# Gated attention and MLP decode: the last product in four column groups of one result row each, copied into one row of 512

## Chip, cores and metric

The kernel runs on 1 core of a Trainium2 chip. The metric is the device time of one execution in microseconds (us); before the change it is 189.38 us (median of 3 runs).

## What is computed

One token of width 512 goes through two branches, which a gate mixes. Branch a is attention with 32 heads of width 128 over a cache of 4096 positions; branch b is an MLP of 1376 units with a squared ReLU. All tensors are bfloat16.

```python
g = sigmoid((x * gate_w).sum(-1, keepdims=True))
q = (x @ wq).reshape(1, 1, 32, 128).transpose(0, 2, 1, 3)
p = softmax(einsum("bhqd,bhkd->bhqk", q, k_cache) * 128 ** -0.5)
o = einsum("bhqk,bhkd->bhqd", p, v_cache)
a = o.transpose(0, 2, 1, 3).reshape(1, 1, 4096) @ wo        # wo: 4096 x 512
r = maximum(x @ w1 + b1, 0)
b = (r * r) @ w2 + b2
out = g * a + (1 - g) * b                                   # 512 numbers
```

## The kernel before

The instructions of each engine are written out by hand, one block for each (SP, GpSimd, ScalarE, TensorE, VectorE), and semaphores order them. The heads are treated in eight groups of four (`NQ = 8`); a group's keys or values are one load of 4 MB, 128 partitions with 32 KB each. SP issues all large loads (wq, w1, w2, the keys and values, and last wo) in one order, each as soon as its buffer is free.

For a group, TensorE transposes a part of the keys (L427), ScalarE copies them, and TensorE forms scores (L441); GpSimd (L313) and VectorE (L680, L689, L695) form the other scores by products and sums. Then come the maximum, the exponentials (L358), the product with the values (L470) and a step that sorts the heads' results out (`extract`, L479). The MLP is computed in the first group's turn.

The steps that matter here are at the ends of the blocks.

- wo lies in SBUF as 128 partitions of 32 rows (`wo_sb[:, t, :]`, t = 0 to 31, 512 columns each). SP loads it in `NW` = 4 pieces, with the bounds `TS`: rows 0-19, 20-27, 28-30 and 31, each with a semaphore of its own (L293).
- `regroup` (L541) and a VectorE copy (L744) bring the attention result, times the gate, into columns: column t of `o2` belongs to row t of wo. `o2` is the middle of three columns per t in `o2p`; the outer two are zeros.
- `accs` are the accumulators of the output, in one PSUM bank (`pX`): two tiles of 2 partitions x 128 columns, at partitions 32 and 0. Column block j of the output (j = 0 to 3) belongs to tile j % 2, and there to partition j // 2. A matmul with a slice of two columns, one of them zero (`o2p[:, t, 1 - j // 2:3 - j // 2]`), adds to one of the two partitions and zero to the other. The bias (L520), the MLP's result (`mlp_cols`, L535) and the rows of wo are added there; for the first two the slice comes from `pick2`, three columns with the middle one set.
- `attn_rows` takes the rows of wo: rows 0 to `WW` - 1 = 15 as one matmul of 512 columns each (L551) into row 0, 32, 64 or 96 of the bank `pO`, and rows 16 to 31 as four matmuls of 128 columns (L557) into `accs`. VectorE copies `pO` to `pvf` (L746), and `wide_rows` (L566) adds its four rows into `accs`, ahead of row 20.
- `busy` (L573) issues matmuls whose results are not used; there are several in the last 17 us, one of them ahead of `wide_rows`.
- After the last matmul VectorE copies tile 0 (L748) and ScalarE tile 1 (L385), each 2 x 128, into `ob`, two partitions of 256, and SP stores these as two rows of 512 bytes (L296).

Of the kernel before, what the change touches and what calls it, by code (L numbers as in the profile page):

```python
# [5 lines left out]
def bass_gated_mix__gqa_block_cached__dense_activation_squared_relu__decode_kernel(  # L6
# [14 lines left out]
    fp32 = mybir.dt.float32  # L21
    i32 = mybir.dt.int32
    bf16 = mybir.dt.bfloat16
    ALU = mybir.AluOpType
    ACT = mybir.ActivationFunctionType
    AX = mybir.AxisListType

    NH = 32
# [39 lines left out]

    TS = [0, 20, 28, 31, 32]
    NW = len(TS) - 1  # L70
    WW = 16


    k_p = A_k_cache.rearrange("a h (q b) d -> (a h q) (b d)", b=NB)
# [2 lines left out]
    wo_v = A_wo.rearrange("(p t) n -> p (t n)", t=32)  # L77
    w1_v = B_w1.rearrange("(p t) n -> p (t n)", t=4)
    w2_v = B_w2[0:F0, :].rearrange("(p g) n -> p (g n)", g=FG)
    out_v = out[0, 0, :].rearrange("(j p) -> j p", p=256)  # L80
    w2_x = B_w2[F1:F, :].rearrange("(q t) n -> q (t n)", t=TX)

    ctx = ExitStack()
    with ctx:
        def sb(name, shape, dt):
            return ctx.enter_context(nc.sbuf_tensor(name, shape, dt))
# [4 lines left out]
        def sem(name):  # L91
            return ctx.enter_context(nc.semaphore(name))
# [8 lines left out]
        wo_sb = WO.rearrange("p (t n) -> p t n", t=32)  # L101
        kT = sb("kT", [128, NR, TC * 128], bf16)
# [9 lines left out]
        grow = sb("grow", [1, DM], bf16)  # L112
        b1r = sb("b1r", [1, F], bf16)

        ob = kT[:, 1, 0:256]
        xcol = sb("xcol", [128, 4], bf16)
        sel = sb("sel", [NH, 4, 128], bf16)
        oT = sb("oT", [NH, 128], bf16)
        o2p = sb("o2p", [128, NH, 3], bf16)
        o2 = o2p[:, :, 1]  # L120
        ident = sb("ident", [128, 128], bf16)
        identf = sb("identf", [128, 128], fp32)
        pick = sb("pick", [128, 4, 60], fp32)
        pvf = sb("pvf", [112, 512], fp32)
# [20 lines left out]
        b2r = Kt[0:1, 2, 14 * 1024:14 * 1024 + DM]  # L145
        b2g = Kt[0:1, 2, 15 * 1024:16 * 1024].bitcast(fp32)

        pick2 = sb("pick2", [112, 3], fp32)

        TT = pb("T", [128, NT * 512], fp32)  # L150
        T = [TT[:, i * 512:(i + 1) * 512] for i in range(NT)]
# [2 lines left out]
        pO = pb("pO", [128, 512], fp32)  # L154
        pM = pb("pM", [128, 512], fp32)
        pX = pb("pX", [128, 512], fp32)
# [5 lines left out]
        SL = pS[0:NH, 0:256].bitcast(bf16)  # L162
        H = pX[:, 160:160 + FN + TX]

        accs = [pX[32:34, 0:128], pX[0:2, 0:128]]
        O = pX[0:NH, 288:416]

        QT = pX[:, :].bitcast(bf16).rearrange("p (j d) -> p j d", d=128)
# [66 lines left out]
        s_wm = sem("s_wm")  # L235
        s_hw = sem("s_hw")
        s_mc = sem("s_mc")
        s_wc = sem("s_wc")
        s_ww = sem("s_ww")
        s_hv = sem("s_hv")  # L240
        s_hs = sem("s_hs")
        s_acc = sem("s_acc")
        s_fin = sem("s_fin")
        s_out = sem("s_out")
# [8 lines left out]
        @on(nc.sync)  # L253
        def _(eng):
            def load_k(i):
                if i >= NK:
                    eng.wait_ge(s_t, CB[i - NK + 1])
                    eng.wait_ge(s_mu, XP * (i - NK + 1))
                    eng.wait_ge(s_pm, GP * (i - NK + 1))  # L259
                if i == 2:  # L260
                    eng.wait_ge(s_ml, 1)
                eng.dma_start(Kt[:, i % NK, :], k_p[i * 128:(i + 1) * 128, :]).then_inc(s_k[i % NK], 16)

            def load_v(i):
                if i == 1:
                    eng.wait_ge(s_qr, NQ)
                    eng.wait_ge(s_h, 2)
                if i < NQ - 2:
                    if i >= NV:
                        eng.wait_ge(s_pv, i - NV + 1)  # L270
                    eng.dma_start(VT(i), v_p[i * 128:(i + 1) * 128, :]).then_inc(s_v[i % NV], 16)
                    return
                eng.wait_ge(s_t, CB[i])
                eng.wait_ge(s_mu, XP * i)
                eng.wait_ge(s_pm, GP * i)
                eng.dma_start(VT(i), v_p[i * 128:(i + 1) * 128, :]).then_inc(s_vl[i - (NQ - 2)], 16)  # L276

            load_k(0)
            eng.dma_start(w1_sb, w1_v).then_inc(s_w1, 16)
            eng.dma_start(w2a, w2_v).then_inc(s_w2, 16)  # L280
            for r in range(4):
                eng.dma_start(WX[r:QX:4, :], w2_x[r:QX:4, :]).then_inc(s_w2, 16)
            load_k(1)
            load_v(0)
            load_k(2)
            for i in range(NQ):
                if i >= 1:
                    load_v(i)
                if i + LAG < NQ:
                    load_k(i + LAG)  # L290
            eng.wait_ge(s_pv, NQ - 3)
            for c in range(NW):
                eng.dma_start(WO[:, TS[c] * DM:TS[c + 1] * DM], wo_v[:, TS[c] * DM:TS[c + 1] * DM])\  # L293
                   .then_inc(s_wo[c], 16)
            eng.wait_ge(s_fin, 2)
            eng.dma_start(out_v, ob[32:34, :]).then_inc(s_out, 16)  # L296
            eng.wait_ge(s_out, 16)

        @on(nc.gpsimd)
# [19 lines left out]
        def _(eng):  # L319
# [62 lines left out]
                    neg_max(i - 1)  # L382
                    exps(i - 1)
            eng.wait_ge(s_acc, 1)
            eng.activation(ob[32:34, 128:256], accs[1], ACT.Copy).then_inc(s_fin, 1)  # L385

        @on(nc.tensor)
        def _(eng):
            eng.wait_ge(s_id, 2)
            for c in range(4):  # L390
                mm = eng.transpose(SL[:, c * 128:c * 128 + 128], ident[:, c:128:4], ident[:, :])
            mm.then_inc(s_sl, 1)
            eng.wait_ge(s_x, 32)
            for t in range(4):
                mm = eng.matmul(XC[:, t:t + 1], xrow[:, t:DM:4], ident[0:1, 0:1], start=True, stop=True)
# [12 lines left out]
            for j in range(NQ):  # L408
                if j >= NT:
                    wait_q(eng, j - NT)  # L410
                for t in range(4):
                    mm = eng.matmul(T[j % NT][:, :], xb[:, t, :], wq_sb[:, t, j * 512:(j + 1) * 512],  # L412
                                    start=(t == 0), stop=(t == 3))
# [99 lines left out]
            def mlp_out():  # L513
                eng.wait_ge(s_w2, 16 * 5)
                eng.wait_ge(s_hs, 1)

                eng.wait_ge(s_wm, 3)
                eng.wait_ge(s_g, 4)
                for j in range(4):
                    eng.matmul(accs[j % 2], pick2[0:1, 1 - j // 2:3 - j // 2], b2g[:, j * 128:j * 128 + 128],  # L520
                               start=(j < 2), stop=False, skip_group_check=True)
                for n in range(FN + TX):
                    if n < FG:
                        rhs = w2a[0:height(n), n * DM:(n + 1) * DM]
                    else:
                        rhs = WX[:, (n - FN) * DM:(n - FN + 1) * DM]
                    r = 32 * (n % 4)
                    mm = eng.matmul(pO[r:r + 1, :], hs[0:height(n), n:n + 1], rhs, start=(n < 4),
                                    stop=(n >= FN + TX - 4))
                mm.then_inc(s_ml, 1)  # L530

            def mlp_cols():
                eng.wait_ge(s_mc, 1)
                for j in range(4):
                    eng.matmul(accs[j % 2], pick2[:, 1 - j // 2:3 - j // 2], pvf[0:112, j * 128:j * 128 + 128],  # L535
                               start=False, stop=False, skip_group_check=True)

            def regroup():
# [7 lines left out]
            def attn_rows(c):  # L546
                eng.wait_ge(s_wo[c], 16)
                for t in range(TS[c], TS[c + 1]):
                    r = 32 * (t % 4)
                    if t < WW:  # L550
                        mm = eng.matmul(pO[r:r + 1, :], o2[:, t:t + 1], wo_sb[:, t, :], start=(t < 4),  # L551
                                        stop=(t >= WW - 4), skip_group_check=True)
                        if t == WW - 1:
                            mm.then_inc(s_ww, 1)
                        continue
                    for j in range(4):
                        mm = eng.matmul(accs[j % 2], o2p[:, t, 1 - j // 2:3 - j // 2],  # L557
                                        wo_sb[:, t, j * 128:(j + 1) * 128], start=False,
                                        stop=(t == 31), skip_group_check=True)
                if c == NW - 1:  # L560
                    mm.then_inc(s_acc, 1)

            def wide_rows():
                eng.wait_ge(s_wc, 1)
                for j in range(4):
                    eng.matmul(accs[j % 2], pick2[:, 1 - j // 2:3 - j // 2], pvf[:, j * 128:(j + 1) * 128],  # L566
                               start=False, stop=False, skip_group_check=True)

            def busy(n):
                for u in range(n):
                    eng.matmul(T[0][:, :], ident[:, :], kT[:, 0, 0:512], start=True, stop=True,  # L573
                               skip_group_check=True)
# [39 lines left out]
            regroup()  # L614
            busy(2)
            for c in range(NW):
                if c == 1:
                    busy(1)
                    wide_rows()
                attn_rows(c)  # L620

        @on(nc.vector)
        def _(eng):
# [9 lines left out]
                              identf[:, :].rearrange("p (c r) -> p c r", c=4)[:, :, 0:16]  # L633
                              .rearrange("p c (b h) -> p b h c", b=4), AX.X, ALU.add).then_inc(s_ho, 1)
            eng.memset(E[:, :, :, :], 0.0).then_inc(s_ho, 1)
            eng.memset(pick2[:, :], 0.0).then_inc(s_wm, 1)
            eng.memset(o2p[:, :, :], 0.0).then_inc(s_wm, 1)
            eng.wait_ge(s_ho, 7)
            eng.wait_ge(s_wm, 2)
            eng.tensor_copy(pick2[:, 1:2], pick[0:112, 0, 28:29]).then_inc(s_wm, 1)  # L640
            eng.wait_ge(s_sl, 1)
            eng.tensor_copy(sel[:, :, :], SL.rearrange("h (c m) -> h c m", c=4)).then_inc(s_ho, 1)
            eng.wait_ge(s_x, 32)
# [98 lines left out]
            eng.tensor_scalar(oT[:, :], O, gcol[0:NH, 0:1], rden[:, 0:1], ALU.mult, ALU.mult).then_inc(s_oc, 1)  # L742
            eng.wait_ge(s_o2, 1)
            eng.tensor_copy(o2[:, :], T[1][:, 0:NH]).then_inc(s_o2, 1)  # L744
            eng.wait_ge(s_ww, 1)
            eng.tensor_copy(pvf[:, :], pO[0:112, :]).then_inc(s_wc, 1)  # L746
            eng.wait_ge(s_acc, 1)
            eng.tensor_copy(ob[32:34, 0:128], accs[0]).then_inc(s_fin, 1)  # L748


# [26 lines left out]
```

## Time and profile before

| | before |
|---|---|
| median of 3 runs | 189.38 us (189.24 to 189.52) |
| profiled execution, time | 189.48 us |
| profiled execution, span from the first to the last instruction | 188.2 us |
| mean granted TensorE clock | 0.70 |
| TensorE matmuls, busy | 109.7 us (58%) |
| TensorE weight loads, busy | 66.2 us (35%) |
| VectorE, busy | 152.9 us (81%) |
| ScalarE, busy | 69.7 us (37%) |
| GpSimd, busy | 137.8 us (73%) |
| read from HBM | 78.33 MB, 416 GB/s over the span |

The profile is of one execution; times in it count from the span's start. The 1.28 us between span and time lie around the profiled instructions. Engines are called PE (TensorE's matmuls), PEld (its weight loads), DVE (VectorE), ACT (ScalarE), POOL (GpSimd) and SP or SPq (the queue that issues loads and stores). L557 is line 557 of the kernel. A form such as `128*2 128x128` is the weights, 128 rows by 2 columns, and the moving data. Shares of busy time say little about the end of a program; what ended last is read from the chain of waits and from the timeline.

### The profile page before, as it was taken

The numbers are of one execution on the slowest core, as the hardware profiler recorded it, in microseconds if no ns is written. First come the engines' busy times: TensorE is split into PE (matmuls) and PEld (weight loads), VectorE is DVE, ScalarE is ACT, GpSimd is POOL, SyncE is SP. The second block draws the span as 40 slices with busy tenths as digits, with TensorE's granted clock in tenths as the row PEclk, the third lists the DMA queues.
The fourth block names the chain that finished last, engine by engine and source line by source line (L and its number), as shares of the span: only waits on it lengthen the run. The fifth ranks groups of instructions, "written<-read, shape, count | busy, mean of one in ns | idle before, by whom it ended". The sixth has DMA issues, their size and how long they took to land. (4 is left out here: it accounts for less than half of the span.)

```text
span 188.2 us, 2612 instructions
## 1 busy us (share of the span) xinstructions
PE 109.7 (58%) x1076; PEld 66.2 (35%) x1078; DVE 152.9 (81%) x127; ACT 69.7 (37%) x170; POOL 137.8 (73%) x38
## 2 busy tenths in 40 slices
PE   1129877787303869146806681858282648458766
PEld 1103352437103628132704181418140634213334
DVE  7112659999997999999999999999999999991022
ACT  3003484208420829404920573055405460506000
POOL 1000199998996999989998999999899989940000
PEclk9999997857655555858665555555557585858999
DMA  7999899999999999999999999999999999999993
GB/s 265 419 432 446 375 438 438 446 425 446 430 432 439 413 425 435 425 446 432 428 425 425 432 439 421 446 432 418 432 428 432 439 425 446 421 418 424 428 394 122
DMA packets 3518, 78.48 MB, mean 417 GB/s; under 512 B 410, under 2 KB 543, under 8 KB 820
## 3 DMA queue, kind: packets, MB, share of 16 engines
q1 hardware_dynamic: 3500, 78.32, 97.3%
q8 instruction: 8, 0.13, 0.3%
q14 instruction: 2, 0.02, 0.0%
q10 hardware_dynamic: 8, 0.01, 0.0%
HBM read 78.33 MB, written 0.00 MB: 416 GB/s over the span
## 5 line engine op out<-in xcount | busy, mean ns | idle before, releaser
L313 POOL TENSOR_TENSOR pg<-Kt,qb 128x2176 f32<-128x2176 bf16 x32 | 137.1, 4317 | 28.4 <-DMA Kt<-in_A_k_cache_dram 23.3
L695 DVE TENSOR_REDUCE Sb<-pg 128x17 f32<-128x2176 f32 x32 | 77.0, 2405 | 2.2 <-POOL pg L313 2.2
L427 PE MATMUL T<-ident,Kt 128*128 128x128 bf16 x256 | 27.6, 294 | 19.2 <-DMA Kt<-in_A_k_cache_dram 19.2
L341 ACT ACTIVATE kT<-T 128x1024 bf16<-128x1024 bf16 x32 | 30.8, 1030 | 17.5 <-PE T L427 17.4
L680 DVE TENSOR_TENSOR pr<-Kt,pQ 128x1792 f32<-128x1792 bf16 x16 | 32.2, 2011 | 1.9 <-DMA Kt<-in_A_k_cache_dram 1.1
L427 PEld LDWEIGHTS T<-ident,Kt 128*128 128x128 bf16 x256 | 24.0, 137 | 23.8 <-DMA Kt<-in_A_k_cache_dram 22.1
L689 DVE TENSOR_REDUCE Sb<-pr 128x14 f32<-128x1792 f32 x16 | 32.1, 2004 | 0.0
L470 PE MATMUL pO<-Vt,E 128*16 128x512 bf16 x192 | 23.0, 576 | 0.5 <-issue 0.5
L358 ACT ACTIVATE E<-Sb,nM 32x128 bf16<-32x128 f32 x32 | 18.7, 583 | 0.9
L351 ACT ACTIVATE nM<-pM 128x4 f32<-128x4 f32 x8 | 1.4, 173 | 46.5 <-PE pM L455 46.5
L441 PE MATMUL pS<-qc,kT 128*128 128x4 bf16 x256 | 11.9, 168 | 8.5 <-ACT kT L341 8.4
L412 PE MATMUL T<-Vt,kT 128*128 128x512 bf16 x32 | 10.0, 454 | 7.8 <-DMA Vt<-in_A_wq_dram 7.8
L451 PE MATMUL pM<-identf,mp 128*1 128x128 f32 x8 | 2.9, 359 | 19.3 <-DVE mp L702 19.3
L441 PEld LDWEIGHTS pS<-qc,kT 128*128 128x128 bf16 x256 | 10.4, 104 | 10.2 <-ACT kT L341 10.1
L479 PE MATMUL pX<-pvf,pick 112*32 112x128 f32 x64 | 12.8, 366 | 1.8 <-ACT pvf L364 1.8
L667 DVE CAST qb<-T 32x128 bf16<-32x128 f32 x12 | 3.4, 287 | 9.2 <-PE T L412 8.9
L333 ACT ACTIVATE qb<-T 32x128 bf16<-32x128 f32 x20 | 5.4, 268 | 14.3 <-PE T L412 13.9
L479 PEld LDWEIGHTS pX<-pvf,pick 112*32 112x32 f32 x64 | 8.6, 146 | 5.2 <-ACT pvf L364 2.5
L470 PEld LDWEIGHTS pO<-Vt,E 128*16 128x16 bf16 x192 | 6.6, 108 | 7.3 <-issue 5.7
L358 ACT ACTIVATION_READ_ACCUMULATOR E<-Sb,nM 32x1 f32 x32 | 8.2, 257 | 0.0
L451 PEld LDWEIGHTS pM<-identf,mp 128*1 128x1 f32 x8 | 0.6, 80 | 20.8 <-DVE mp L702 20.6
L455 PE MATMUL pM<-gm,onesf 1*128 1x4 f32 x16 | 4.1, 322 | 6.5 <-DVE gm L706 6.5
(81 smaller groups left out, 76.3 us busy)
## 6 DMA issues: line engine op xcount, KB each, us to landing
Kt<-in_A_k_cache_dram SPq DMA_DIRECT2D x8, 4096.0 KB, 31.2
Vt<-in_A_v_cache_dram SPq DMA_DIRECT2D x6, 4096.0 KB, 31.0
Kt<-in_A_v_cache_dram SPq DMA_DIRECT2D x2, 4096.0 KB, 31.6
Vt<-in_A_wq_dram SPq DMA_DIRECT2D x1, 3840.0 KB, 11.8
Vt<-in_A_wo_dram SPq DMA_DIRECT2D x1, 2560.0 KB, 33.2
Kt<-in_B_w_dram SPq DMA_DIRECT2D x1, 1376.0 KB, 23.9
Kt<-in_B_w_dram SPq DMA_DIRECT2D x1, 1280.0 KB
Vt<-in_A_wo_dram SPq DMA_DIRECT2D x1, 1024.0 KB, 35.2
```

What stands on the lines that cost most here:

```text
L313: eng.tensor_tensor(pg[:, n % 2, 0:g, :], Kt[:, i % NK, k * g * 128:(k + 1) * g * 128] .rearrange("p (b d) -> p b d", b=g), qb[:, i:i + 1, ...
L333: eng.activation(qb[a:b, j, :], T[j % NT][a:b, h * 128:(h + 1) * 128], ACT.Copy)\
L341: eng.activation(kT[:, n % NR, :], T[n % NT][:, :].bitcast(bf16), ACT.Copy).then_inc(s_ev, 1)
L358: eng.activation(E[a:b, j % NE, :, h], Sb[a:b, j % NS, :], ACT.Exp, bias=nM[a:b, 4 * j + h:4 * j + h + 1], scale=SCALE, accum_out=RS[a:b, ...
L412: mm = eng.matmul(T[j % NT][:, :], xb[:, t, :], wq_sb[:, t, j * 512:(j + 1) * 512], start=(t == 0), stop=(t == 3))
L427: mm = eng.transpose(T[n % NT][:, :].bitcast(bf16)[:, y * 128:(y + 1) * 128], Kt[:, i % NK, w * 128:(w + 1) * 128], ident[:, :])
L441: mm = eng.matmul(S[:, c * TC + y, :], kT[:, n % NR, y * 128:(y + 1) * 128], qc[:, 4 * i:4 * i + 4], start=True, stop=True)
L470: mm = eng.matmul(pO[r:r + 16, :], E[:, i % NE, 4 * y:4 * y + 4, :], VT(i)[:, y * 512:(y + 1) * 512], start=(y < 4), stop=(y >= NG - 4))
L479: mm = eng.matmul(O, pick[0:112, b, 28 - 4 * i:60 - 4 * i], pvf[:, b * 128:(b + 1) * 128], start=False, stop=(i == NQ - 1 and b == 3), ski ...
L680: eng.tensor_tensor(pr[:, 0:x, :], Kt[:, i % NK, a * 128:(a + x) * 128] .rearrange("p (b d) -> p b d", b=x), PQ[:, i % 4:i % 4 + 1, :].bro ...
L689: eng.tensor_reduce(Sb[:, i % NS, a:a + x], pr[:, 0:x, :], AX.X, ALU.add).then_inc(s_sd, 1)
L695: eng.tensor_reduce(Sb[:, i % NS, k * g:(k + 1) * g], pg[:, n % 2, 0:g, :], AX.X, ALU.add)\
```

## The change

All 32 rows of wo are taken as four matmuls of 128 columns, and each column block has a result row of its own: `accs[j]` is one partition, 32 * j, in one of the four column groups. The weights of a matmul are then one column, so the zero columns of `o2p` and `pick2` go, with the memsets and the wait that set them. The wide rows, VectorE's copy of them, `wide_rows` and one `busy` matmul go too. At the end VectorE copies blocks 0 and 1 and ScalarE blocks 2 and 3 into one partition of 512 columns, and SP stores it as one row of 1 KB. The pieces in which wo is loaded stay.

```diff
-    WW = 16
...
-    out_v = out[0, 0, :].rearrange("(j p) -> j p", p=256)
+    out_v = out[0, :, :]
...
-        ob = kT[:, 1, 0:256]
+        ob = kT[0:1, 1, 0:512]
...
-        o2p = sb("o2p", [128, NH, 3], bf16)
-        o2 = o2p[:, :, 1]
+        o2 = sb("o2", [128, NH], bf16)
...
-        pick2 = sb("pick2", [112, 3], fp32)
+        pick2 = sb("pick2", [112, 1], fp32)
...
-        accs = [pX[32:34, 0:128], pX[0:2, 0:128]]
+        accs = [pX[32 * j:32 * j + 1, 0:128] for j in range(4)]
...
-            eng.wait_ge(s_fin, 2)
-            eng.dma_start(out_v, ob[32:34, :]).then_inc(s_out, 16)
+            eng.wait_ge(s_fin, 4)
+            eng.dma_start(out_v, ob[:, :]).then_inc(s_out, 16)
...
-            eng.activation(ob[32:34, 128:256], accs[1], ACT.Copy).then_inc(s_fin, 1)
+            for j in range(2, 4):
+                eng.activation(ob[:, j * 128:(j + 1) * 128], accs[j], ACT.Copy).then_inc(s_fin, 1)
...
                 for j in range(4):
-                    eng.matmul(accs[j % 2], pick2[0:1, 1 - j // 2:3 - j // 2], b2g[:, j * 128:j * 128 + 128],
-                               start=(j < 2), stop=False, skip_group_check=True)
+                    eng.matmul(accs[j], pick2[0:1, :], b2g[:, j * 128:j * 128 + 128],
+                               start=True, stop=False, skip_group_check=True)
...
-                    eng.matmul(accs[j % 2], pick2[:, 1 - j // 2:3 - j // 2], pvf[0:112, j * 128:j * 128 + 128],
+                    eng.matmul(accs[j], pick2[:, :], pvf[0:112, j * 128:j * 128 + 128],
                                start=False, stop=False, skip_group_check=True)
...
                 for t in range(TS[c], TS[c + 1]):
-                    r = 32 * (t % 4)
-                    if t < WW:
-                        mm = eng.matmul(pO[r:r + 1, :], o2[:, t:t + 1], wo_sb[:, t, :], start=(t < 4),
-                                        stop=(t >= WW - 4), skip_group_check=True)
-                        if t == WW - 1:
-                            mm.then_inc(s_ww, 1)
-                        continue
                     for j in range(4):
-                        mm = eng.matmul(accs[j % 2], o2p[:, t, 1 - j // 2:3 - j // 2],
+                        mm = eng.matmul(accs[j], o2[:, t:t + 1],
                                         wo_sb[:, t, j * 128:(j + 1) * 128], start=False,
                                         stop=(t == 31), skip_group_check=True)
...
-            def wide_rows():
-                eng.wait_ge(s_wc, 1)
-                for j in range(4):
-                    eng.matmul(accs[j % 2], pick2[:, 1 - j // 2:3 - j // 2], pvf[:, j * 128:(j + 1) * 128],
-                               start=False, stop=False, skip_group_check=True)
...
             for c in range(NW):
-                if c == 1:
-                    busy(1)
-                    wide_rows()
                 attn_rows(c)
...
-            eng.memset(pick2[:, :], 0.0).then_inc(s_wm, 1)
-            eng.memset(o2p[:, :, :], 0.0).then_inc(s_wm, 1)
             eng.wait_ge(s_ho, 7)
-            eng.wait_ge(s_wm, 2)
-            eng.tensor_copy(pick2[:, 1:2], pick[0:112, 0, 28:29]).then_inc(s_wm, 1)
+            eng.tensor_copy(pick2[:, :], pick[0:112, 0, 28:29]).then_inc(s_wm, 1)
...
-            eng.wait_ge(s_ww, 1)
-            eng.tensor_copy(pvf[:, :], pO[0:112, :]).then_inc(s_wc, 1)
             eng.wait_ge(s_acc, 1)
-            eng.tensor_copy(ob[32:34, 0:128], accs[0]).then_inc(s_fin, 1)
+            for j in range(2):
+                eng.tensor_copy(ob[:, j * 128:(j + 1) * 128], accs[j]).then_inc(s_fin, 1)
```

More of the change, by code (lines that the diff above doesn't have):

```diff
@@ L237, in bass_gated_mix__gqa_block_cached__dense_activation_squared_relu__decode_kernel @@
         s_mc = sem("s_mc")
-        s_wc = sem("s_wc")
-        s_ww = sem("s_ww")
         s_hv = sem("s_hv")
@@ L515, in mlp_out @@
                 eng.wait_ge(s_hs, 1)
-                eng.wait_ge(s_wm, 3)
+                eng.wait_ge(s_wm, 1)
                 eng.wait_ge(s_g, 4)
                 for j in range(4):
-                    eng.matmul(accs[j % 2], pick2[0:1, 1 - j // 2:3 - j // 2], b2g[:, j * 128:j * 128 + 128],
-                               start=(j < 2), stop=False, skip_group_check=True)
+                    eng.matmul(accs[j], pick2[0:1, :], b2g[:, j * 128:j * 128 + 128],
+                               start=True, stop=False, skip_group_check=True)
                 for n in range(FN + TX):
```

## Prediction

> **What bounds the kernel now.** I read the chain of waits first, because one number is wanted: which work ended last. Its last pieces (start, duration, what):
>
> ```profile
> 149.84 35.22 DMA Vt<-in_A_wo_dram
> 185.05 0.04 issue
> 185.10 1.57 PE pX L557 x48
> 186.67 0.02 issue
> 186.69 0.28 DVE kT L748
> ```
>
> The kernel streams 78 MB, and the end hangs on the load of wo. The reader should see that TensorE starts 0.04 us after a landing and that only the last 1.9 us before the store (187.00) are not transfer. Next the view of the transfers (size, us from issue to landing), since wo comes in four pieces:
>
> ```profile
> Vt<-in_A_wo_dram SPq DMA_DIRECT2D x1, 1024.0 KB, 35.2
> Vt<-in_A_wo_dram SPq DMA_DIRECT2D x1, 384.0 KB, 35.7
> ...
> Vt<-in_A_wo_dram SPq DMA_DIRECT2D x1, 128.0 KB, 35.5
> ```
>
> The first piece, 2560 KB, takes 33.2. They are issued at 149.36, 149.84, 150.30 and 150.78, so rows 0-19 are there at 182.56, rows 20-27 at 185.05, 28-30 at 186.00, row 31 at 186.32. Nothing in the change touches this stream, so 186.32 is my fixed point. Then the timeline of the tail (start, duration, engine, line), TensorE first, then the last copies and the store:
>
> ```profile
> 182.61 1.03 PE L551 MATMUL pO<-Vt,o2p 128*1 128x512 bf16 x16 [0.55 <-DMA Vt<-in_A_wo_dram]
> 183.47 0.61 PE L557 MATMUL pX<-Vt,o2p 128*2 128x128 bf16 x16
> 184.01 0.39 PE L573 MATMUL T<-kT,ident 128*128 128x512 bf16 x1
> 184.44 0.61 PE L566 MATMUL pX<-pvf,pick 112*2 112x128 f32 x8
> 185.10 1.55 PE L557 MATMUL pX<-Vt,o2p 128*2 128x128 bf16 x48
> ```
>
> ```profile
> 186.69 0.27 ACT L385 ACTIVATE kT<-pX 2x128 bf16<-2x128 f32 x1 [12.57 <-PE pX L557]
> 186.69 0.28 DVE L748 CAST kT<-pX 2x128 bf16<-2x128 f32 x1 [2.31 <-PE pX L557]
> 187.00 0.29 SPq L296 DMA_DIRECT2D out_dram<-kT  x1
> ```
>
> All that the change takes out (VectorE's copy L746, 0.69 us from 183.69, and L566 and one L573) lies before 185.05, under the wait for rows 20-27. The last copies run side by side, one on each engine.
>
> **The matmuls.** Now two column groups work at a time: in the trace the two matmuls of a pair start 0.003 us apart and pairs follow every 0.056 us. Four groups of 128 columns are not in the trace. From below, a row of four takes 0.056: the wide rows run in four groups, their four matmuls start within 0.01 us and the next four follow 0.215 later, so the groups overlap. From above, 0.112: no more matmuls per us than the pairs reach. I take 0.056, since four groups at once is the nearer row. Either way 20 rows from 182.61 cost 1.1 to 2.2 us and end by 185.05: hidden under the transfer (without that cover the second figure would cost 1.1). Rows 20-27 take 0.45 (at most 0.9) of the 0.94 us until rows 28-30 land. At the end only row 31 counts: it lands at 186.32, its weights load at 186.36, its four matmuls start by 186.37. Now its last pair starts at 186.43, queued behind the pairs of rows 28-30, and ends 0.22 later, at 186.65. So at full clock TensorE ends 0.065 us earlier, at 186.585.
>
> **The clock.** The change also thins out TensorE's work: L566's passes and a filler matmul go, 20 rows end at about 183.9, and then it idles until 185.05. The granted clock changes in steps of 3.41 us. A view by such stretches (TensorE's busy us first, granted clock third from the end):
>
> ```profile
> 27.59:31.00 3.41, 2.19 (x33) 1.16 (x31) 3.41 (x2) 2.84 (x7) 3.41 (x1) 1.00 1.17 498
> 31.01:34.41 3.40, 3.40 (x11) 1.06 (x9) 3.40 (x3) 0.00 (x0) 3.40 (x2) 0.50 0.99 424
> 44.66:48.07 3.41, 2.31 (x50) 1.66 (x47) 3.32 (x4) 2.89 (x7) 2.98 (x1) 1.00 1.05 452
> 48.08:51.48 3.40, 0.58 (x2) 0.50 (x2) 3.40 (x3) 0.92 (x4) 3.40 (x2) 0.50 1.03 431
> 177.78:181.19 3.41, 2.76 (x31) 1.37 (x20) 1.10 (x3) 0.00 (x0) 0.00 (x0) 1.00 0.97 410
> 181.19:184.60 3.41, 2.56 (x39) 1.15 (x41) 0.90 (x2) 0.00 (x0) 0.00 (x0) 1.00 0.90 368
> ```
>
> At full clock a stretch with 2.19 or 2.31 us of matmuls was followed by half clock, one with 2.76 by full clock, and so was the last one shown, with 2.56 (1.00 from 184.60 to 188.02 too). In 181.19 to 184.60 the changed kernel has 0.60 (the two fillers ahead of the rows) and 1.28 (19 steps of 0.056 and 0.22): 1.88 us, below both that fell. So I expect 0.50 from about 184.6. At 0.50 the steps double to 0.107: rows 20-27 last until 186.15, just past the landing of rows 28-30; these start at 186.04, 186.15, 186.25, and row 31 at 186.37. A 128x128 matmul on this page takes 0.314 at half clock (L427's median) against 0.217: TensorE ends at 186.68, 0.03 later than now instead of 0.065 earlier.
>
> The Trainium skill ("TensorE: Matmul & The Clock Gate", Part 1 and the table of what matters for kernels) states that the clock falls after a whole idle window of about 3.4 us and stays up without idle gaps over about 3 us. By that rule no drop comes, for the longest pause here is 1.2 us. The rows above disagree with it: the stretch from 44.66 has 2.31 us of matmuls in it and half clock followed.
>
> **The copies.** Each engine now copies two pieces one after the other instead of one. 1x128 in succession is not in the trace; the nearest rows are four 32x128 casts from PSUM in a row:
>
> ```profile
> 16.71 1.24 DVE L667 CAST qb<-T 32x128 bf16<-32x128 f32 x4 [6.74 <-PE T L412]
> 15.00 1.14 ACT L333 ACTIVATE qb<-T 32x128 bf16<-32x128 f32 x4 [9.51 <-PE T L412]
> ```
>
> One takes 0.28 (VectorE) or 0.27 (ScalarE), so each further one adds about 0.31 to 0.32, or 0.29. The last copy, with 2 partitions, took 0.28 as the ones with 32 do, so fewer partitions save nothing. VectorE sets the end: +0.31 (0.32 at most; 0.21 if the second overlaps the first by 0.07 as some neighbours at the start do). Nothing covers it, since the store waits for all four. Nothing is queued behind on either engine, and on SP behind the store only the final wait.
>
> **The store.** Two rows of 512 B become one of 1 KB. Packets of 512 B took 0.027 us, of 1 KB (wo's last piece) 0.046; the second of the two now starts 0.019 after the first, so one row ends when both do now. Issuing took 0.29 for two rows, 0.21 to 0.52 for the one-row loads at the start. I take 0, between -0.07 and +0.23; the landing is the rest of 1.2 us and stays.
>
> **What costs nothing.** VectorE loses memsets (0.06, 0.14) and a wait near 3 us; behind them, at 16.71, it waits 6.74 us for TensorE (0.2 if that cover were gone). The bias and MLP matmuls in four groups instead of two save at most 0.2 us near 38 and 47 us, where loads on SP wait for TensorE, but with 31 us from issue to landing the stream doesn't see it.
>
> **The sum.** +0.03 (matmuls at half clock) + 0.31 (second copy) + 0 = +0.34 us. The profiled execution (span 188.2, 1.28 around it, 189.48) becomes 189.82; it lies 0.10 over the median 189.38, so the median becomes 189.72.
>
> **Rivals.**
> The clock stays at full: -0.065 + 0.31 = +0.245, 189.62. For it: the steps of 3.41 us need not lie as in this execution, and one stretch with 2.17 us (24.18 to 27.59) was followed by full clock. Against it: the rows above. This is what the skill's rule would give.
> The copies overlap fully on each engine: -0.065 to +0.03, 189.32 to 189.41, no change. For it: at the start of the program a memset begins at 2.84 while its forerunner runs to 2.89. Against it: none of the casts from PSUM overlaps.
> Slower by far: TensorE waits for its own code. The page counts 8 instruction packets on q8; in the trace they hold 16 KB, take 1.02 to 1.10 us, and lie 215 to 293 of TensorE's instructions apart, 251 in mean. After the eighth, at 180.11, 191 instructions are left now. The change adds 48 matmuls with their loads, removes 8 with theirs and a filler: +78, so 269. From about 251 on a ninth block may be needed, in rows 28 to 31. If it is, and TensorE waits one packet, the end moves by 1.07: 190.8. Against it: 18 instructions past a mean may well lie inside the block, and no wait now coincides with a fetch.
>
> **Numbers.** Half clock 0.52, full clock 0.20, overlapping copies 0.10, code 0.08, other longer tails (four groups slower than assumed, a dearer store) 0.10. A measurement here tells 0.2% from no change, 0.38 us: the lines are 189.00 and 189.76. The likeliest case lies 0.04 below the upper one, its terms reach further up (0.32, 0.23) than down, and medians move by 0.1: I put 0.28 of its 0.52 above. With 0.04 of the full clock, the code and the other tails: slower 0.50. Faster gets 0.03, from overlapping copies with a cheaper store; the rest, 0.47, is no change. The half-clock case alone spans 189.55 to 189.95. The range, 189.40 to 190.25, takes in the full clock, the upper side of the overlap and the dearer tails, and leaves out waiting for code.
>
> **What would show it.** In the new profile: the last wo piece still lands near 186.3; 128 one-column matmuls for the rows, four per 0.056 us (0.107 after about 184.6 if the clock fell); TensorE's last end between 186.58 and 186.68; two copies per engine, 0.31 and 0.29 apart; the store issued near 187.35. I am wrong if the copies overlap, if a row of four takes over 0.11 us at full clock, if a gap that nothing in the profile releases opens in the last rows, or if the landing of wo moves.

## The result, and the profile after

The median after the change is 189.65 us (22 runs, 189.45 to 189.88), against 189.38 us before (22 runs on the same chip, 189.21 to 189.65). The ratio is 1.0015, 95% interval 1.0009 to 1.0022: slower by 0.15%, 0.27 us. The forecast was 189.72. The profiled execution took 189.74 us with a span of 188.4, so it lies 0.09 over the median, as the one before did by 0.10.

The chain of waits of the changed kernel, its last pieces (start, duration, what):

```profile
150.58 35.42 DMA Vt<-in_A_wo_dram
185.99 0.04 issue
186.04 0.57 PE pX L547 x16
186.61 0.02 issue
186.63 0.28 DVE kT L723
186.91 0.03 issue
186.94 0.28 DVE kT L723
```

The transfer still sets the start of the tail. What is new is the last line: a second copy in series. The transfers of wo, now the second to fourth piece, with size and time from issue to landing:

```profile
Vt<-in_A_wo_dram SPq DMA_DIRECT2D x1, 1024.0 KB, 35.0
Vt<-in_A_wo_dram SPq DMA_DIRECT2D x1, 384.0 KB, 35.4
Vt<-in_A_wo_dram SPq DMA_DIRECT2D x1, 128.0 KB, 35.3
```

The last packet of the last piece lands at 186.308, against 186.319 before: the fixed point held. The timeline of TensorE in the tail of the changed kernel (start, duration, what, in brackets the idle time before and what ended it):

```profile
182.61 1.29 PE L547 MATMUL pX<-Vt,o 128*1 128x128 bf16 x80 [0.59 <-DMA Vt<-in_A_wo_dram]
185.11 0.62 PE L547 MATMUL pX<-Vt,o 128*1 128x128 bf16 x32 [1.21 <-DMA Vt<-in_A_wo_dram]
186.04 0.54 PE L547 MATMUL pX<-Vt,o 128*1 128x128 bf16 x16 [0.31 <-DMA Vt<-in_A_wo_dram]
```

The last x16 are rows 28 to 31, and the wait for row 31 lies within them. It shows in the same timeline at the loading of row 31's weights (PEld):

```profile
186.35 0.09 PEld L547 LDWEIGHTS pX<-Vt,o 128*1 128x1 bf16 x4 [0.16 <-DMA Vt<-in_A_wo_dram]
```

Twenty rows (80 matmuls) take 1.29 us, so they end 1.2 us before rows 20-27 land. TensorE waits for each of the three later pieces; the wo transfer, not TensorE, orders the tail. The last copies and the store, in the same timeline:

```profile
186.63 0.56 ACT L382 ACTIVATE kT<-pX 1x128 bf16<-1x128 f32 x2 [12.65 <-PE pX L547]
186.63 0.59 DVE L723 CAST kT<-pX 1x128 bf16<-1x128 f32 x2 [5.27 <-PE pX L547]
187.25 0.28 SPq L292 DMA_DIRECT2D out_dram<-kT  x1
```

The two engines still work side by side, but each line now holds two copies. The instructions behind them show VectorE's second copy starting at 186.941, 0.310 after its first, and ScalarE's 0.294 after its first. The store is issued at 187.250 instead of 187.005, and the span ends at 188.408 instead of 188.163: +0.245 us.

The clock, by stretches of the changed kernel (window, its us, then busy us and instructions of PE, PEld, DVE, ACT, POOL; then the granted clock, the DMA share and GB/s):

```profile
180.41:183.83 3.42, 2.08 (x86) 1.37 (x86) 0.59 (x2) 0.00 (x0) 0.00 (x0) 1.00 0.91 377
183.83:187.24 3.41, 1.23 (x56) 0.67 (x48) 0.56 (x2) 0.54 (x2) 0.00 (x0) 1.00 0.36 134
```

The clock stayed at 1.00 past the last matmul, after a stretch with only 2.08 us of matmuls. That is the full-clock rival.

### The profile page after: what moved, and what is told of

It reads as the page before. It is cut to its first block, busy times and chain, and to the rows that moved or that the text cites. A ratio compares the mean times of both kernels' runs of the same rounds, so it can differ in the third digit from the quotient of the medians.

```text
span 188.4 us, 2688 instructions
## 1 busy us (share of the span) xinstructions
PE 109.2 (58%) x1115; PEld 65.7 (35%) x1117; DVE 152.4 (81%) x125; ACT 70.0 (37%) x171; POOL 137.7 (73%) x38
## 5 line engine op out<-in xcount | busy, mean ns | idle before, releaser
L467 PE MATMUL pO<-Vt,E 128*16 128x512 bf16 x192 | 23.5, 583 | 0.2 <-issue 0.2
L476 PE MATMUL pX<-pvf,pick 112*32 112x128 f32 x64 | 13.6, 385 | 1.6 <-ACT pvf L360 1.6
L409 PE MATMUL T<-Vt,kT 128*128 128x512 bf16 x32 | 9.4, 442 | 7.8 <-DMA Vt<-in_A_wq_dram 7.8
L476 PEld LDWEIGHTS pX<-pvf,pick 112*32 112x32 f32 x64 | 9.1, 153 | 5.5 <-ACT pvf L360 2.5
```

The source lines that it names most:

```text
L467: mm = eng.matmul(pO[r:r + 16, :], E[:, i % NE, 4 * y:4 * y + 4, :], VT(i)[:, y * 512:(y + 1) * 512], start=(y < 4), stop=(y >= NG - 4))
L476: mm = eng.matmul(O, pick[0:112, b, 28 - 4 * i:60 - 4 * i], pvf[:, b * 128:(b + 1) * 128], start=False, stop=(i == NQ - 1 and b == 3), ski ...
```

## The experiments

My theory: the change costs one more copy in series (+0.31) and saves the queue of pairs ahead of row 31 (-0.065); nothing else matters. Its rivals: the cost is in the four column groups or in the lost wide rows, in TensorE's clock, in TensorE's code, or in the store's form. All runs are set against the kernel before, run on the same chip each time (medians 189.38 to 189.44). Since the last landing differs from execution to execution by up to 0.37 us, I read each trace by two distances from it, to the issue of the store and to the end of the span:

| kernel | median us | ratio to before (95%) | landing to issue of store | landing to end |
|---|---|---|---|---|
| before | 189.38 | - | 0.686 | 1.844 |
| after | 189.65 | 1.0015 (1.0009 to 1.0022) | 0.942 | 2.100 |
| e1 all rows in pairs | 189.47 | 1.0001 (0.9992 to 1.0009) | 0.692 | 1.852 |
| e2 one copy per engine | 189.90 | 1.0025 (1.0015 to 1.0035) | 0.633 | 2.300 |
| e3 VectorE copies four | 190.32 | 1.0046 (1.0033 to 1.0059) | 1.578 | 2.731 |
| e4 two-row form | 189.69 | 1.0014 (1.0005 to 1.0023) | 0.942 | 2.103 |
| e5 no fillers | 189.74 | 1.0014 (1.0005 to 1.0022) | 0.992 | 2.150 |
| e6 more instructions | 189.77 | 1.0019 (1.0010 to 1.0027) | 1.133 | 2.293 |
| e7 before, copies halved | 189.52 | 1.0004 (0.9995 to 1.0014) | 0.759 | 1.921 |
| e8 more fillers | 189.73 | 1.0015 (1.0006 to 1.0023) | 0.943 | 2.102 |
| e9 after, copies halved | 189.87 | 1.0025 (1.0014 to 1.0036) | 1.074 | 2.232 |
| e10 adjacent rows in the store | 189.50 | 1.0003 (0.9994 to 1.0012) | 0.631 | 1.845 |
| e11 rows at edges of groups | 189.50 | 1.0003 (0.9994 to 1.0012) | 0.648 | 1.810 |

**e1: the matmuls alone.** All 32 rows as pairs in the kernel before, its two copies and its store kept.

```diff
-    WW = 16
+    WW = 0
...
-                if c == 1:
-                    busy(1)
-                    wide_rows()
...
-            eng.wait_ge(s_ww, 1)
-            eng.tensor_copy(pvf[:, :], pO[0:112, :]).then_inc(s_wc, 1)
```

> The kernel before with its old accumulators, copies and store, but all 32 rows of wo in pairs (no wide rows, no copy of them, one filler less). The copies theory (the change costs the second copy in series, 0.31 us, less 0.065 us that TensorE ends earlier): the matmuls of the first pieces are hidden, so no change, within 0.05 us of the kernel before; 20 rows end by about 185.0, rows 28 to 31 in pairs as now, TensorE's last end 0.06 to 0.07 us later after the last landing than in the changed kernel, store issued 0.69 us after that landing. The matmul theory (taking out the wide rows and the filler is what costs): slower by 0.2 to 0.3 us.

The time is that of before (ratio 1.0001). The timeline of e1:

```profile
182.51 4.04 PE L557 MATMUL pX<-Vt,o2p 128*2 128x128 bf16 x128 [0.20 <-DMA Vt<-in_A_wo_dram]
186.59 0.28 DVE L743 CAST kT<-pX 2x128 bf16<-2x128 f32 x1 [4.93 <-PE pX L557]
186.90 0.29 SPq L296 DMA_DIRECT2D out_dram<-kT  x1
```

128 matmuls in two groups fill the time up to the last landing and cost nothing, so the lost wide rows and the lost `busy` matmul are not what costs: how the first 31 rows are computed does not matter, as long as they are done when row 31 lands. TensorE's last end lies 0.338 behind the landing, as before (0.333); in after it is 0.271, and that is what the four groups save. The loss of the change is behind TensorE.

**e3: two more copies.** VectorE copies all four blocks, ScalarE none.

```diff
-            for j in range(2, 4):
-                eng.activation(ob[:, j * 128:(j + 1) * 128], accs[j], ACT.Copy).then_inc(s_fin, 1)
...
-            for j in range(2):
+            for j in range(4):
                 eng.tensor_copy(ob[:, j * 128:(j + 1) * 128], accs[j]).then_inc(s_fin, 1)
```

> The changed kernel with all four 1x128 copies on VectorE, none on ScalarE. The copies theory: each copy in series costs the same 0.31 us, so 0.62 us more than the changed kernel, 0.87 over before: about 190.25, starts 0.31 apart. If what costs is the two engines sharing a bank, it is less than that.

The copies and the store in the timeline of e3:

```profile
186.61 1.23 DVE L720 CAST kT<-pX 1x128 bf16<-1x128 f32 x4 [4.98 <-PE pX L544]
187.87 0.28 SPq L292 DMA_DIRECT2D out_dram<-kT  x1
```

Four copies start 0.31 us apart. The store comes 1.578 after the landing, 0.636 later than with two. The median is 0.89 over that of before, where after is 0.27 over it: 0.62 more. The time follows the number of copies in series, at 0.31 each.

**e2: one copy again.** From after: VectorE copies partitions 0 to 63, which hold two of the result rows, and ScalarE 64 to 127; the store takes partitions 0, 32, 64 and 96.

```diff
-    out_v = out[0, :, :]
+    out_v = out[0, 0, :].rearrange("(j p) -> j p", p=128)
...
-        ob = kT[0:1, 1, 0:512]
+        ob = kT[:, 1, 0:128]
...
-            eng.wait_ge(s_fin, 4)
-            eng.dma_start(out_v, ob[:, :]).then_inc(s_out, 16)
+            eng.wait_ge(s_fin, 2)
+            eng.dma_start(out_v, ob[0:128:32, :]).then_inc(s_out, 16)
...
-            for j in range(2, 4):
-                eng.activation(ob[:, j * 128:(j + 1) * 128], accs[j], ACT.Copy).then_inc(s_fin, 1)
+            eng.activation(ob[64:128, :], pX[64:128, 0:128], ACT.Copy).then_inc(s_fin, 1)
...
-            for j in range(2):
-                eng.tensor_copy(ob[:, j * 128:(j + 1) * 128], accs[j]).then_inc(s_fin, 1)
+            eng.tensor_copy(ob[0:64, :], pX[0:64, 0:128]).then_inc(s_fin, 1)
```

> The changed kernel with its matmuls as they are, but one copy per engine: VectorE takes the partitions 0 to 63 of the accumulator bank, ScalarE 64 to 127, 128 columns each, and the store takes the four result rows of 256 B from partitions 0, 32, 64 and 96. The copies theory: the 0.31 us are gone, the store is issued about 0.62 us after the last landing, so 0.31 us less than the changed kernel and 0.06 less than before: 189.3. The matmul theory: still 0.2 to 0.3 us over before. If stores of 256 B rows land later, part of the gain goes there: then issue to landing is over 1.15 us.

The tail in the timeline of e2:

```profile
186.53 0.27 ACT L381 ACTIVATE kT<-pX 64x128 bf16<-64x128 f32 x1 [12.41 <-PE pX L546]
186.53 0.28 DVE L721 CAST kT<-pX 64x128 bf16<-64x128 f32 x1 [5.28 <-PE pX L546]
186.84 0.58 SPq L292 DMA_DIRECT2D out_dram<-kT  x1
```

Half of the expectation held: the store is issued 0.633 after the landing, 0.31 sooner than in after and 0.05 sooner than before. But the kernel got slower, since the store takes 0.58 to issue instead of 0.28, and 1.67 from issue to the end of the span instead of 1.16. Two theories for that: four rows are dear, or rows 32 partitions apart are.

**e10: four adjacent rows.** e2 with another slice in the store. It leaves out three of the four result rows, so its output is not that of the kernel; only the store's time is wanted.

```diff
-            eng.dma_start(out_v, ob[0:128:32, :]).then_inc(s_out, 16)
+            eng.dma_start(out_v, ob[0:4, :]).then_inc(s_out, 16)
```

> The changed kernel with one copy per engine as in the run with four result rows of 256 B, but the store takes four adjacent partitions, 0 to 3, instead of 0, 32, 64 and 96; so three of the four rows of the output are left out and others stand in their place. It measures the store's form alone. The stride theory (a step of 32 partitions between the rows is what made that store slow: 0.585 us to issue, 1.65 from issue to the end): issued in 0.29, end 1.15 later, 0.06 us under the kernel before. The row theory (rows of 256 B are slow): as slow as with the stride, 0.45 over before.

The timeline of e10:

```profile
186.76 0.28 DVE L721 CAST kT<-pX 64x128 bf16<-64x128 f32 x1 [5.51 <-PE pX L546]
187.07 0.31 SPq L292 DMA_DIRECT2D out_dram<-kT  x1
```

Four adjacent rows cost 0.31 to issue and 1.21 to the end: the partition step is what costs, about 0.28 in the issue and 0.45 in all. The trace before already had such rows, which I had not looked at: four loads into every fourth partition take far longer to issue than the 0.21 to 0.52 of the one-row loads at the start. They also move more (25 KB against 2.7 KB at most), so they only point the same way (the source view of that line, min/median/max in ns):

```profile
L282 SPq DMA_DIRECT2D Kt<-in_B_w_dram x4: 657/672/809, 3.2 to 5.5; - x4
```

**e11: one copy and a plain store.** From after: the four result rows lie at partitions 31, 32, 95 and 96, so that a copy of 64 partitions holds two neighbours. For 31 and 95 the weights are 32 columns of which only the last is not zero.

```diff
-        o2 = sb("o2", [128, NH], bf16)
+        o2p = kT[:, 2, :].rearrange("p (t c) -> p t c", c=32)
+        o2 = o2p[:, :, 31]
...
-        accs = [pX[32 * j:32 * j + 1, 0:128] for j in range(4)]
+        accs = [pX[0:32, 0:128], pX[64:96, 0:128], pX[32:33, 0:128], pX[96:97, 0:128]]
+        WC = [0, 0, 31, 31]
...
-                        mm = eng.matmul(accs[j], o2[:, t:t + 1],
+                        mm = eng.matmul(accs[j], o2p[:, t, WC[j]:32],
...
-            eng.dma_start(out_v, ob[:, :]).then_inc(s_out, 16)
+            eng.dma_start(out_v, ob[31:33, :]).then_inc(s_out, 16)
...
+            eng.activation(ob[0:64, 128:256], pX[64:128, 0:128], ACT.Copy).then_inc(s_fin, 1)
...
+            eng.tensor_copy(ob[0:64, 0:128], pX[0:64, 0:128]).then_inc(s_fin, 1)
```

> The changed kernel with its four column groups, but the result rows at the partitions 31, 32, 95 and 96 (the first and third group get weights of 32 columns of which only the last is set), so that one copy per engine of 64 partitions puts them into two adjacent partitions of 256 columns, and the store is two rows of 512 B as in the kernel before. The zeros are set on VectorE at about 171 us, where it waits. The copies theory: TensorE ends 0.065 us earlier than before, one copy each, the same store: 0.05 to 0.07 us under before, 0.3 under the changed kernel. If weights of 32 columns slow the rows, TensorE's end moves later by as much as its last row.

The timeline of e11:

```profile
186.13 0.55 PE L548 MATMUL pX<-Vt,kT 128*32 128x128 bf16 x16 [0.31 <-DMA Vt<-in_A_wo_dram]
186.75 0.27 ACT L383 ACTIVATE kT<-pX 64x128 bf16<-64x128 f32 x1 [12.34 <-PE pX L548]
186.75 0.28 DVE L728 CAST kT<-pX 64x128 bf16<-64x128 f32 x1 [5.09 <-PE pX L548]
187.06 0.29 SPq L294 DMA_DIRECT2D out_dram<-kT  x1
```

It keeps what the four groups save and has no second copy: 0.648 from landing to issue, 0.038 less than before. Its time can't be told from that of before (1.0003, 0.9994 to 1.0012): the median is 0.06 over, where that of after is 0.27 over. So the loss of the change goes with the second copy. The gain of 0.05 to 0.07 that I had expected over before did not show. The trace has 0.03, because the copies start 0.058 after TensorE's end instead of 0.042, and that is too small for this measurement; I found no kernel that is faster than both.

**e7 and e9: do two copies overlap?** e7 cuts each last copy of the kernel before into two of 64 columns; e9 does so with each of the four copies of after (VectorE's part is shown, ScalarE's is alike).

```diff
e7
-            eng.tensor_copy(ob[32:34, 0:128], accs[0]).then_inc(s_fin, 1)
+            for h in range(2):
+                eng.tensor_copy(ob[32:34, 64 * h:64 * h + 64], accs[0][:, 64 * h:64 * h + 64]).then_inc(s_fin, 1)
e9
-                eng.tensor_copy(ob[:, j * 128:(j + 1) * 128], accs[j]).then_inc(s_fin, 1)
+                for h in range(2):
+                    a = j * 128 + 64 * h
+                    eng.tensor_copy(ob[:, a:a + 64], accs[j][:, 64 * h:64 * h + 64]).then_inc(s_fin, 1)
```

> The kernel before with each of its two last copies cut in two of 64 columns, one after the other on the same engine. Nothing else changes. The copies theory: the cost is one instruction in series, mostly a fixed part: a second copy of half the length adds 0.22 to 0.26 us less the 0.07 that the shorter first one saves; 0.15 to 0.2 us over before. If it is the length that costs, no change.

The timeline of e7:

```profile
186.64 0.32 ACT L386 ACTIVATE kT<-pX 2x64 bf16<-2x64 f32 x2 [12.38 <-PE pX L559]
186.64 0.35 DVE L751 CAST kT<-pX 2x64 bf16<-2x64 f32 x2 [2.31 <-PE pX L559]
187.02 0.29 SPq L296 DMA_DIRECT2D out_dram<-kT  x1
```

A copy of 64 columns takes 0.21, yet two end after 0.35: the second starts 0.145 after the first (0.12 on ScalarE), before the first has ended. In the trace the store is issued 0.073 later than before, instead of the 0.15 to 0.2 that I had expected; the median's 0.08 is within the noise. So copies from PSUM can overlap, which my prediction had denied. In e7 both halves lie in the same partitions; in after, the second copy reads another one. e9 has both kinds in a row.

> The changed kernel with each of its four last copies cut in two of 64 columns: each engine copies two halves of one result row (same partition), then two halves of the next (32 partitions on). The partition theory (two copies in a row overlap where they start at the same partition and do not where the start moves, as in the kernel before with halved copies, 0.12 to 0.15 us apart, against 0.31 in the changed kernel): steps of about 0.14, 0.24, 0.14 us on VectorE. The length theory (short copies overlap, those of 128 columns do not): 0.14 for all three. In time within 0.15 us of the changed kernel.

The timeline of e9, and its first two VectorE copies alone (a window that ends behind the second's start):

```profile
186.60 0.68 ACT L384 ACTIVATE kT<-pX 1x64 bf16<-1x64 f32 x4 [12.51 <-PE pX L549]
186.60 0.72 DVE L727 CAST kT<-pX 1x64 bf16<-1x64 f32 x4 [5.28 <-PE pX L549]
187.35 0.28 SPq L292 DMA_DIRECT2D out_dram<-kT  x1
```

```profile
186.60 0.34 DVE L727 CAST kT<-pX 1x64 bf16<-1x64 f32 x2 [5.28 <-PE pX L549]
```

VectorE's four start at 186.597, .738, .971 and 187.116, so 0.141, 0.233 and 0.145 apart; ScalarE's steps are 0.124, 0.224 and 0.126. The two halves of one row overlap. From row to row, where the partition that is read moves by 32, the step is longer than the copy, which takes 0.20 to 0.22. What in the hardware makes that difference, the runs do not show.

**e5 and e8: the clock.** e5 leaves out the `busy` matmuls around the last `extract` and `regroup` of after, to bring the clock down; e8 adds four `busy` matmuls ahead of row 20, to keep it up.

```diff
e5
-            busy(3)
             extract(NQ - 1)
-            busy(1)
             regroup()
-            busy(2)
e8
             for c in range(NW):
+                if c == 1:
+                    busy(4)
                 attn_rows(c)
```

> The changed kernel without the six filler matmuls around the last sorting step and the regrouping (three, one and two), so that TensorE does less between 178.4 and 182.6 us. The clock theory (less work lets the granted clock fall to half for the last rows): the clock is 0.50 from 184 us at the latest, the last four matmuls take 0.31 us each instead of 0.22, and the time is 0.09 us over the changed kernel, so 0.34 over before. If the clock stays at full, the changed kernel's time.

The last two stretches of e5 (columns as above), and its matmuls of wo by source (durations min/median/max in ns, first and last start):

```profile
180.24:183.65 3.41, 1.29 (x80) 1.22 (x84) 0.59 (x2) 0.00 (x0) 0.00 (x0) 1.00 0.95 392
183.66:187.00 3.34, 1.88 (x68) 1.09 (x53) 0.37 (x2) 0.38 (x2) 0.00 (x0) 0.50 0.43 164
```

```profile
L547 PE MATMUL pX<-Vt,o x128: 216/220/315, 182.6 to 186.3; 128*1 128x128 bf16 x128
```

The clock fell at 183.66 (I had expected about 184.6 in after), and the distance from landing to issue grew by only 0.05: the last matmul takes 0.264 at half clock, not the 0.314 of my row. In the instructions behind that view the later rows of a burst take 0.31, but the first row after a pause 0.262 to 0.268, and row 31 is one of those. The time is that of after (1.0014 against 1.0015).

> The changed kernel with four filler matmuls of 512 columns after rows 0 to 19, where TensorE waits 1.2 us for the next piece. The clock theory: they hold the clock at full, so whatever the changed kernel loses to half clock in its executions comes back, up to 0.09 us. The copies theory with the clock at full anyway: no change against the changed kernel, 0.25 over before.

e8's trace shows full clock in both stretches, and 189.73 us (1.0015) is the time of after again. I have read the clock of the tail in one execution of each kernel; whatever it is in the others, here it moves the median by less than can be seen.

**e6: TensorE's code.** 48 matmuls of one column ahead of the last groups' products, to move the fetch of the ninth block of instructions.

```diff
             busy(2)
+            for u in range(48):
+                eng.matmul(T[0][0:1, 0:1], ident[:, 0:1], ident[:, 0:1], start=True, stop=True,
+                           skip_group_check=True)
```

> The changed kernel with 48 more tiny matmuls (1x1, with their loads: 96 instructions) near 172.4 us, where TensorE waits for the exponentials. They bring the fetch of TensorE's ninth 16 KB block forward, from 186.3 us (after the last packets of wo) to about 183 to 185. The copies theory: the block is ahead of need, no change unless it lands on one of the transfer engines that finish late; at most 0.05 us. The code theory (a fetch near the end holds up the last landing of wo or TensorE): up to 1.1 us slower, with the last landing of wo later than 186.4.

It missed its aim. The ninth packet still came at 186.29. The additional work, in an execution whose clock stayed at 0.50 until 179.17 (170.17 in after), delayed all that follows on TensorE. The timeline of e6:

```profile
184.75 1.96 PE L547 MATMUL pX<-Vt,o 128*1 128x128 bf16 x128
```

The rows start 2.1 us later than in after and run without a wait until 186.71, 0.46 after the last landing instead of 0.27. On the code it is inconclusive. It shows how far TensorE can be late: about 2 us, then the tail pays.

**e4: the store's form.** The store of after written as two rows of 512 B.

```diff
-    out_v = out[0, :, :]
+    out_v = out[0, :, :].rearrange("o (j p) -> o j p", j=2)
...
-            eng.dma_start(out_v, ob[:, :]).then_inc(s_out, 16)
+            eng.dma_start(out_v, ob.rearrange("o (j p) -> o j p", j=2)).then_inc(s_out, 16)
```

> The changed kernel with its one row of 512 columns stored as two rows of 512 B instead of one of 1 KB. The copies theory: the form of the store is worth nothing, within 0.03 us from issue to landing, so the time of the changed kernel. The store theory (one row on one queue lands later than two on two): 0.1 us or more faster than the changed kernel, with the landing that much nearer to the issue.

In the trace the transfer is again one row of 1 KB: the two adjacent rows were merged, so this was the kernel after once more (1.0014, landing to end 2.103). It says nothing of the form, but repeats the result. For the form there are the traces of before (two rows) and after (one row): 1.158 from issue to end in both.

## Why the prediction was right, and where it was not

- **The fixed point** held: wo's last piece lands at 186.308 (forecast near 186.3).
- **The matmuls** came out at the lower bound: four per 0.056 us, and with the full clock TensorE's last end is 186.579 (forecast 186.585). e1 shows that the cover that I named is real, since even twice the price lies under the transfer.
- **The copies** have the size forecast: 0.310 and 0.294 apart against 0.31 and 0.29. e2, e3 and e11 show that this is the cost of the change. The reason that I gave was wrong. Copies from PSUM do overlap where they stay in the same partitions (e7, e9), and the trace before had shown it: ScalarE's copies L341 read all 128 partitions each time, and the first four, from 25.91, take 1.02 to 1.04 each but start 0.90 to 0.92 apart. The four casts of my rows moved by 32 partitions, as the copies of the change do. The prediction did not name that likeness, so the right figure is in part luck.
- **The store** was taken at 0 for one row instead of two: issue 0.28 against 0.29, issue to end 1.158 in both.
- **The clock** is the step that failed. I took 0.50 from 184.6, because 1.88 us of matmuls lay below two stretches that were followed by half clock. The profiled execution's stretch began 0.8 us earlier than I had laid it, held 2.08 us, still less than the 2.19 and 2.31 that fell, and full clock followed. It is not only where the stretch lies: in e2, which has the matmuls of after, one lies at 181.19 to 184.61, as I had laid it, with 1.89 us, and the clock stayed at 1.00 until 188.02; e9 (from 181.35) and e10 (from 181.12) show the same with 1.89. So busy time of matmuls in a stretch does not decide alone. The Trainium skill ("TensorE: Matmul & The Clock Gate", Part 1) has the clock fall after an idle window of about 3.4 us. The profile after agrees, with no pause over 1.21 us; e5 does not, since its clock fell at 183.66 with no pause over 1.57. What decides stays open.
- **The size of that step** was wrong too. I took half clock to cost 0.09 at the end (186.68 against 186.585), from the 0.314 of matmuls in a row; for a row after a pause e5 shows 0.05. So the term of +0.03 (half clock) was -0.073 with the clock as the trace has it, and would be -0.02 at half clock by e5's price.
- **The sum.** -0.073 (TensorE's end, 186.579 against 186.652) + 0.31 (second copy) + 0.01 (the copies start 0.052 after that end instead of 0.042) = +0.245, the full-clock rival's figure; the store was issued at 187.250, not near 187.35. That the rival is met to the last digit is luck: the landing came 0.011 earlier in this execution, which hides the 0.01 that nobody had counted. Read from the landing the sum is -0.062 + 0.31 + 0.01, 0.256 in all. The median moved by 0.27, so the forecast of 189.72 was 0.07 too high, and the rival's 189.62 too low by 0.03. The forecast came this near because the step that failed is worth only 0.1 beside the copy's 0.31. By its own lines (189.00 and 189.76) 189.65 is no change, to which it gave 0.47, against 0.50 for slower.
- **The code rival** was counted rightly, but no wait followed. The page of the profile of after has a ninth packet (queue and kind, then packets, MB, share of 16 engines):

```profile
q8 instruction: 9, 0.15, 0.3%
```

It starts at 186.26 and takes 1.32 us, eight instructions before TensorE's last, and no wait shows: row 31's weights load 0.04 after its landing, as before. The packet ends at 187.58, a microsecond after TensorE's last end, so none of its matmuls waited for what it brought. e1 has nine packets too and loses nothing, but its ninth starts at 186.63, after TensorE's last end. Whether TensorE waits for a packet that it needs stays open.

## What to carry to other kernels

Behind the last landing, count the instructions in series on each engine: here one more copy of 128 numbers costs 0.31 us of a 189 us kernel, while 128 matmuls under the transfer cost nothing. A copy of 64 partitions takes the 0.28 us of a copy of one, so gather PSUM rows by partitions rather than by more copies, and place the rows so that the store needs no partition step. Here that only won back what the second copy had cost (e11).

## What the runs showed of the hardware

- In these runs two copies from PSUM in a row on one engine overlap if they read the same partitions (steps of 0.145 and 0.12 us at 64 columns, where a copy takes about 0.21; 0.90 to 0.92 on ScalarE for 128x1024, which takes 1.02 to 1.04); if the partition that is read moves by 32 they do not (0.233 and 0.224; 0.310 and 0.294 at 128 columns). The partition alone is not the whole rule: in before VectorE's cast L661, which reads SBUF from partition 0, starts 0.08 before the end of the last of four casts L667, which reads PSUM from partition 96.
- A store of four rows of 256 B that are 32 partitions apart takes 0.58 us to issue, and 1.67 from issue to the end of the span; of four adjacent rows 0.31 and 1.21.
- A matmul with one column of weights and 128 of moving data takes 0.22 us at full clock; at half clock 0.31, but only 0.262 to 0.268 in the first row after a pause (e5).
